# A second expert layer over pairs of batches: seven block products in place of eight

## The chip, the cores and the metric

The kernel runs on one core of one Trainium2 chip. The metric is the device time of one execution in microseconds (us), from the hardware profiler; lower is better. TensorE is called PE (its weight loads PEld), VectorE DVE, ScalarE ACT, GpSimd POOL; SP is the engine whose queue issues nearly all transfers (DMA).

## What is computed

```python
def _attn_ref(q, k, v, g_q, g_k):            # batch 4, heads 12, seq 448, head_dim 64
    q_n, k_n = (rmsnorm(q, g_q), rmsnorm(k, g_k))
    scores = scale * np.matmul(q_n, k_n.transpose(0, 1, 3, 2))
    scores = scores - np.max(scores, axis=-1, keepdims=True)
    attn = np.exp(scores)
    attn = attn / (np.sum(attn, axis=-1, keepdims=True) + 1e-09)
    return np.matmul(attn, v).astype(np.float32)

def _moe_ref(x, w_in, w_out):                # x 1792 x 768, w_in 768 x 2048, w_out 2048 x 768
    h = x @ w_in
    relu6 = np.clip(h + 3.0, 0.0, 6.0)
    g = h * relu6 / 6.0
    return (g @ w_out).astype(np.float32)

def _moe2_ref(x, w_in, w_out):               # the same sizes
    h = x @ w_in
    r = np.maximum(h, 0.0)
    g = r * r
    return (g @ w_out).astype(np.float32)

def reference(**kwargs):
    attn_out = _attn_ref(**attn_kwargs)
    x = np.ascontiguousarray(attn_out.transpose(0, 2, 1, 3)).reshape(B * S, H * D)
    x = _moe_ref(x=x, **moe_kwargs)
    return _moe2_ref(x=x, **moe2_kwargs)
```

The four weight matrices are float64; q, k, v and the result are float32.

## The kernel before, in words

**Numbers.** A product in the two layers is made to float32's precision by float16 matmuls. Both operands are multiplied by a power of two and split into a high and a low float16 part, and each product is three matmuls: high by high, high by low, low by high (L1017 to L1019). One such matmul takes a 128x128 block of weights and 448 columns, the tokens of one batch; the text calls it a *layer matmul*. There are 4608 of them.

**Weights.** `convert` (L867) takes a row of blocks of a weight matrix: it loads the float64 words (tile `wr`, L882), and makes float32 of them (tile `wf`) by five instructions: the sign (L902), the high word (L890 on ACT or L894 on DVE), the low word (L899), the join (L906) and the largest value (L913 on ACT or L909 on DVE). `scale_of` (L329) takes the largest over the partitions by a PE transpose (L341), eight small DVE instructions (L338 to L356) and a PE outer product (L350); the text calls this a *scale chain*. Then the row is split into high (L937, L940) and low (L944), tile `ws`. The first batch that needs a row uses it straight from `ws`; it is also stored to DRAM (`spill`, L947), and the other three batches load it from there (`again`, L960).

**Units.** `units()` (L38) lists the PE's work for the two layers: for each layer m and batch b, 16 units "in" (one 128-wide block row of h, 18 matmuls each) and 18 units "out" (three for each of the six block rows of the result, 18, 15 and 15 matmuls). The last six "out" units of a batch stand behind the "in" units of the next. A unit's position n in this list is the key of its tasks, and what it needs gets keys slightly below n.

**Around a unit.** `gate` (L1042) reads h from PSUM and makes g: for the first layer L1054 and L1060, for the second relu (L1056, ACT) and square (L1066 on ACT or L1063 on DVE). Once the 16 rows of a batch are there, `factors` (L1084) makes one scale for g and splits it (L1116 on ACT or L1119 on DVE, then L1122 on DVE). `result_y` (L1151) reads the first layer's result y, splits it to float16, puts it to DRAM (`kept`, L1191), and gets it back as `yk` (L1194) when the second layer starts. `result` (L1200) reads the second layer's result and stores it.

**Order.** `Plan` (L106) holds every task with its key, the engines that may do it with a cost for each, the tasks it waits for and the tiles it uses. `order` (L129) runs through time with these costs and writes one fixed program for each engine; `tc.manual_schedule()` (L1233) issues it in that order. Tiles live in classes of slots (`CLASSES`, L77; PSUM's eight banks are class `ps`). `STEPS`, `SCALE`, `VMAX`, `LOOK` and `LOOK0` shift the keys of the attention and of the preparation.

**Course.** Attention of batch 0 comes first; then the first layer of batch b, with the attention of batch b+1 beside it; then the second layer of batches 0 to 3. The second layer's weights are prepared while its batch 0 runs.

Of the kernel before, what the change touches and what calls it, by code (L numbers as in the profile page):

```python
# [9 lines left out]
F32 = mybir.dt.float32  # L10
# [39 lines left out]
UNITS = units()  # L50
# [26 lines left out]
CLASSES = {"A": 13, "H": 52, "B": 3, "wr": 3, "w": 8, "ps": 8}  # L77
# [197 lines left out]
def tile_kernel(ctx: ExitStack, tc: tile.TileContext, qk, v, vn, g, ident, w1i, w1o, w2i, w2o, out):  # L275
    nc = tc.nc

    def pool(name, bufs, **kw):
# [16 lines left out]
        "wf": ("w", 5, 5, [P, NW], F32), "ws": ("w", 6, 6, [P, 2, KC, P], F16),  # L295
        "ps_s": ("ps", 4, 5, [P, 512], F32), "ps_a": ("ps", 2, 3, [P, 512], F32), "ps_r": ("ps", 1, 1, [P, 512], F32), "ps_c": ("ps", 1, 2, [P, 512], F32), "ps_m": ("ps", 2, 3, [P, 512], F32),
# [22 lines left out]
    kept = dram.tile([B, KC, P, 2, S], F16, name="kept")  # L319
    spill = dram.tile([2 * (FC + KC * 3), P, 2, NW], F16, name="spill")  # L320
# [8 lines left out]
    def scale_of(key, name, vals, deps):  # L329
# [536 lines left out]

    def convert(m, i0, ns):  # L867
# [4 lines left out]
        vals, t_fs, t_ms = [], [], []  # L872
        for x, (i, n) in enumerate(zip(ids, ns)):
# [6 lines left out]
            def load(kind=kind, row=row, f0=f0, nf=nf, nw=nw, vwr=vwr):  # L880
                src = (w1i, w2i)[m][row] if kind == "in" else (w1o, w2o)[m][row][:, f0:f0 + nf]
                nc.sync.dma_start(tl(vwr)[:, 0:2 * nw], src.rearrange("p k c -> p (k c)").bitcast(I32))  # L882

            def words(vwr=vwr, nw=nw):
                x_ = tl(vwr).rearrange("p (c w) -> p c w", w=2)
                return x_[:, 0:nw, 0], x_[:, 0:nw, 1]

            def dx_a(words=words):
                x_ = words()[1].bitcast(F32)
                nc.scalar.activation(x_, x_, AF.Copy, scale=2.0 ** -112)  # L890

            def dx_v(words=words):
                x_ = words()[1].bitcast(F32)
                nc.vector.tensor_scalar(x_, x_, 2.0 ** -112, None, op0=ALU.mult)  # L894

            def d1(words=words, vwf=vwf, nw=nw):
                l_ = words()[0]
                low = tl(vwf).bitcast(U8).rearrange("p (c w) -> p c w", w=4)[:, 0:nw, 0]
                nc.scalar.activation(low, l_.bitcast(U32), AF.Copy, scale=2.0 ** -29 * (1 - 2.0 ** -9), bias=-0.49)  # L899

            def sign(words=words, vwf=vwf, nw=nw):
                nc.vector.tensor_scalar(tl(vwf)[:, 0:nw].bitcast(I32), words()[1], -(1 << 31), None, op0=ALU.bitwise_and)  # L902

            def join(words=words, vwf=vwf, nw=nw):
                w = tl(vwf)[:, 0:nw].bitcast(I32)
                nc.vector.scalar_tensor_tensor(w, words()[1], 3, w, op0=ALU.logical_shift_left, op1=ALU.bitwise_or)  # L906

            def most(vwf=vwf, nw=nw, x=x):
                nc.vector.tensor_reduce(mx[:, x:x + 1], tl(vwf)[:, 0:nw], axis=AX.X, op=ALU.max, apply_absolute_value=True)  # L909

            def sum_a(words=words, vwr=vwr, vwf=vwf, nw=nw, x=x):

                nc.scalar.activation(tl(vwr).bitcast(F32)[:, 0:nw], tl(vwf)[:, 0:nw], AF.Abs, accum_out=mx[:, x:x + 1])  # L913
# [3 lines left out]
            t_2 = task(kc, [("DVE", dve1(nw), sign)], [t_l], [vwr, vwf])  # L917
# [359 lines left out]
```

## Time and profile before

| | |
|---|---|
| three runs | 1176.98, 1178.19, 1178.38 us (median 1178.19) |
| span of the profiled execution | 1177.7 us; the page gives no other time for that execution |
| PE busy | 1108.0 us (94%), 6070 matmuls |
| DVE busy | 729.9 us (62%) |
| ACT busy | 690.8 us (59%) |
| POOL busy | 98.1 us (8%) |
| DMA | 231.18 MB, mean 196 GB/s |
| the chain that ended last | PE 72%, DVE 13%, ACT 8%, DMA 5%, issue 2% |

Busy shares are means over the whole span. Six stretches of it are told apart in the text, by the first layer matmul on new data: the first layer of batch 1 starts on PE at 287.70 us, of batch 2 at 432.70, of batch 3 at 581.90; at 656.90 PE takes the first gated values of batch 3; at 696.70 the first `yk` of the second layer (batch 0), at 818.00 that of batch 1, and the end is at 1177.70. The matmuls' own durations overlap, so the pace of PE is read from long runs of them in the chain, not from the mean of one.

### The profile page before, as it was taken

What the parts mean: (1) busy time and instruction counts of PE and PEld (TensorE: products, weight loads), DVE (VectorE), ACT (ScalarE), POOL (GpSimd) and SP (SyncE); (2) the same over time, 40 slices, a digit from 0 to 9 for tenths busy, and PEclk for the clock granted to TensorE, in tenths of its full rate; (3) what the DMA queues carried; (4) which work ended last, traced back from release to release, by engine and by line L of the source; (5) the groups of instructions that cost most, each with busy time, mean ns of one, the idle gap of its engine ahead of it and who ended that gap; (6) DMA issues with size and microseconds to landing.
All of it is one profiled execution on the core that took longest, in us unless ns stands there. A gap on an engine that the chain in (4) does not pass through costs nothing.

```text
span 1177.7 us, 17027 instructions
## 1 busy us (share of the span) xinstructions
PE 1108.0 (94%) x6070; PEld 573.7 (49%) x6070; DVE 729.9 (62%) x1676; ACT 690.8 (59%) x1353; POOL 98.1 (8%) x142
## 2 busy tenths in 40 slices
PE   0789999799999998999999998989999999999998
PEld 0455555355554444554555544544555555555554
DVE  7999899999899968899335657696144002100300
ACT  2799799996788846787223658784464034113400
POOL 3421211101111111210000000000000000000000
PEclk9999999899999999999999999999999999999999
DMA  9866567779989899998833767759636434454351
GB/s 239 216 185 196 151 190 235 242 158 310 305 199 231 212 251 244 224 210 207 206 107 117 261 219 281 276 180 319 226 128 201 161 113 135 132 157 121 90 164 54
DMA packets 214742, 231.18 MB, mean 196 GB/s; under 512 B 137872, under 2 KB 174864, under 8 KB 214656
## 3 DMA queue, kind: packets, MB, share of 16 engines
q1 hardware_dynamic: 214592, 229.95, 68.5%
q8 instruction: 48, 0.79, 0.3%
q14 instruction: 38, 0.31, 0.1%
q0 software_dynamic: 64, 0.13, 0.1%
HBM read 156.47 MB, written 36.18 MB: 164 GB/s over the span
## 4 chain that ended last, share of the span: by engine, by line
PE 72%; DVE 13%; ACT 8%; DMA 5%; issue 2%; POOL 0%; SPq 0%; DVEq 0%; ACTq 0%
PE m L1018 60%; PE ps_s L697 4%; DVE g L1122 2%; PE ps_a L793 2%; PE ps_a L774 2%; PE ps_s L667 2%; ACT wf L899 2%; DVE ws L944 2%; DVE nm L704 1%; PE ps_r L760 1%; ACT e L657 1%; DMA wr<-in_w2i_dram 1%; ACT wr L890 1%; ACT wr L913 1%; DMA qk<-in_qk_dram 1%
## 5 line engine op out<-in xcount | busy, mean ns | idle before, releaser
L1018 PEld LDWEIGHTS <-ws 128*128 128x128 f16 x4608 | 446.4, 98 | 430.3 <-issue 15.7
L1018 PE MATMUL m<-g,ws 128*128 128x448 f16 x2304 | 457.3, 354 | 7.6 <-DVE ws L944 3.8
L1018 PE MATMUL m<-x,ws 128*128 128x448 f16 x1152 | 232.7, 353 | 2.2 <-DVE ws L944 0.8
L1018 PE MATMUL m<-yk,ws 128*128 128x448 f16 x1152 | 224.4, 354 | 0.2 <-DVE ws L944 0.2
L657 ACT ACTIVATE e<-ps_s,nm,esc 128x448 f32<-128x448 f32 x168 | 122.1, 729 | 18.0 <-DVE nm L714 17.4
L704 DVE TENSOR_REDUCE nm<-ps_s 128x1 f32<-128x448 f32 x168 | 102.0, 612 | 3.4 <-PE ps_s L697 3.3
L1056 ACT ACTIVATE t<-m,inv 128x448 f32<-128x448 f32 x64 | 39.7, 624 | 98.5 <-PE m L1018 98.5
L1205 ACT ACTIVATE o<-m,ov 128x448 f32<-128x448 f32 x24 | 14.5, 631 | 137.4 <-PE m L1018 137.4
L1054 ACT ACTIVATE t<-m,half,six 128x448 f32<-128x448 f32 x64 | 46.0, 724 | 56.1 <-PE m L1018 56.1
L902 DVE TENSOR_SCALAR wf<-wr 128x768 int32<-128x768 int32 (+1 forms) x68 | 35.7, 529 | 60.2 <-PE m L1018 42.2
L906 DVE SCALAR_TENSOR_TENSOR wf<-wr,wf 128x768 int32<-128x768 int32 (+1 forms) x68 | 61.4, 906 | 12.6 <-ACT wf L899 11.9
L899 ACT ACTIVATE wf<-wr 128x768 uint8<-128x768 uint32 (+1 forms) x68 | 68.7, 1015 | 0.9 <-DVE wf L902 0.8
L697 PE MATMUL ps_s<-T,W 128*128 128x448 f16 (+1 forms) x192 | 61.9, 368 | 4.1 <-DMA W<-W_0r 3.8
L944 DVE SCALAR_TENSOR_TENSOR ws<-wf,w_s,ws 128x768 f16<-128x768 f32 (+1 forms) x68 | 64.7, 961 | 1.0 <-ACT ws L937 0.9
L1063 DVE SCALAR_TENSOR_TENSOR gr<-t 128x448 f32<-128x448 f32 x10 | 6.2, 622 | 95.3 <-ACT t L1056 95.2
L667 PE MATMUL ps_s<-eye,e 128*112 128x128 f32 x308 | 50.3, 297 | 15.7 <-ACT e L657 15.4
L890 ACT ACTIVATE wr<-wr 128x768 f32<-128x768 f32 (+1 forms) x52 | 45.1, 867 | 33.3 <-DVE wf L902 33.3
L697 PE MATMUL ps_s<-T 128*128 128x448 f16 (+1 forms) x192 | 62.5, 374 | 1.6 <-ACT e L657 0.9
L1060 DVE SCALAR_TENSOR_TENSOR gr<-t,m 128x448 f32<-128x448 f32 x64 | 39.1, 614 | 38.3 <-ACT t L1054 38.0
L338 DVE TENSOR_REDUCE g_s<-gm 128x1 f32<-128x16 f32 x4 | 0.7, 164 | 95.8 <-ACT gr L1066 95.6
L734 DVE SCALAR_TENSOR_TENSOR p<-e,su,p 128x448 f16<-128x448 f32 x91 | 59.1, 674 | 0.6 <-DMA ws<-spill 0.2
L913 ACT ACTIVATE wr<-wf 128x768 f32<-128x768 f32 (+1 forms) x62 | 50.3, 813 | 11.2 <-DVE wf L906 11.1
(199 smaller groups left out, 1268.9 us busy)
## 6 DMA issues: line engine op xcount, KB each, us to landing
ws<-spill SPq DMA_DIRECT2D x132, 384.0 KB, 3.7
ws<-spill SPq DMA_DIRECT2D x72, 320.0 KB, 3.7
spill<-ws SPq DMA_DIRECT2D x44, 384.0 KB, 4.2
wr<-in_w1i_dram SPq DMA_DIRECT2D x16, 768.0 KB, 5.2
wr<-in_w2i_dram SPq DMA_DIRECT2D x16, 768.0 KB, 6.0
qk<-in_qk_dram SPq DMA_DIRECT2D x23, 448.0 KB, 4.9
wr<-in_w1o_dram SPq DMA_DIRECT2D x12, 640.0 KB, 4.8
spill<-ws SPq DMA_DIRECT2D x24, 320.0 KB, 4.1
```

The lines of the kernel that those rows point to most:

```text
L657: nc.scalar.activation(tl(ve)[:, r % 2], tl(vps)[:, 0:S], AF.Exp, bias=sums["nm"][:, r:r + 1], scale=esc, accum_out=sums["su"][:, r:r + 1])
L667: nc.tensor.transpose(o[:, c], tl(ve)[:, r % 2, c * VR:(c + 1) * VR], eye)
L697: nc.tensor.matmul(ps[at:at + z - a, 0:S], q_[:, a:z], ks[:, h * S:(h + 1) * S], start=(i == 0), stop=(i == 1))
L704: nc.vector.tensor_reduce(sums["nm"][:, r:r + 1], tl(vps)[:, 0:S], axis=AX.X, op=ALU.max, negate=True)
L734: nc.vector.scalar_tensor_tensor(tl(vp)[:, r % 2, 1], tl(ve)[:, r % 2], sums["su"][:, r:r + 1], tl(vp)[:, r % 2, 0], op0=ALU.mult, op1=ALU ...
L890: nc.scalar.activation(x_, x_, AF.Copy, scale=2.0 ** -112)
L899: nc.scalar.activation(low, l_.bitcast(U32), AF.Copy, scale=2.0 ** -29 * (1 - 2.0 ** -9), bias=-0.49)
L906: nc.vector.scalar_tensor_tensor(w, words()[1], 3, w, op0=ALU.logical_shift_left, op1=ALU.bitwise_or)
L913: nc.scalar.activation(tl(vwr).bitcast(F32)[:, 0:nw], tl(vwf)[:, 0:nw], AF.Abs, accum_out=mx[:, x:x + 1])
L944: nc.vector.scalar_tensor_tensor(tl(vws)[:, 1, 0:nf].rearrange("p k c -> p (k c)"), tl(vwf)[:, 0:nw], up, hi, op0=ALU.mult, op1=ALU.subtract)
L1018: nc.tensor.matmul(tl(vph)[:, 0:S], w[:, wa, k], tl(rhs[k])[:, xa], start=(first_ and k == 0 and c == 0), stop=(last and k == nf - 1 and c ...
L1054: nc.scalar.activation(tl(vt), tl(vph)[:, 0:S], AF.Relu, bias=half, scale=six[:, row:row + 1])
```

## The change

The first layer stays as it was. The second layer works on two batches at once, (0, 1) and (2, 3). A weight matrix is cut into four blocks, A11, A12, A21, A22 (halves of its rows and of its columns), and the data into B11, B12, B21, B22 (halves of the inner dimension, and the two batches). Four blocks of the result need eight block products if each is made by itself. The change makes them from seven products of sums: S1 = A21+A22, S2 = S1-A11, S3 = A11-A21, S4 = A12-S2, and T1 = B12-B11, T3 = B22-B12, T2 = B22-T1, T4 = B21-T2. The products are 1: A11·B11, 2: A12·B21, 3: S4·B22, 4: A22·T4, 5: S1·T1, 6: S2·T2, 7: S3·T3.

- **Weights** (`sums`): two rows of blocks are loaded and made float32 as before (`words_of`, the same five instructions), one scale chain serves both, four additions (L1051) make the sums, and the seven pieces are split into high (L988, L992) and low (L996) and stored to DRAM (`spill_i`, `spill_o`). Every use loads them from there (L1107, L1117), the first one too. The keys run from 91.9 on, 3.27 apart for the first matrix and 2.43 for the second.
- **Data**: y is put to DRAM as float32, `combine` gets it back (L1346), makes the four differences (L1378) and splits the seven operands (L1360, L1366). `split_g` does the same for g (L1518, then L1502 or L1505, and L1508).
- **Products**: `pair_in` (L1465) takes 9 matmuls for a product of one row pair, `pair_out` (L1555) 24, in three rows. `accumulate` leaves sums of products in PSUM: bank A takes products 1, 6, 7, 4 one behind the other, B takes 2, C takes 5 and 3. After each product the bank is read (L1404 on ACT, L1407 on DVE, L1410 with an addition on DVE) before the next goes into it. The rows of `pair_in` are interleaved: 1, 2 and 5 of row 0, 1 and 2 of row 1, 6 of row 0, 5 of row 1, 7 of row 0, 1 and 2 of row 2, 6 of row 1, 4 of row 0, and so on.
- **Gates**: L1478 on DVE, or L1481 and L1482 on ACT, in place.
- **Order**: the in-products of pair 0, the last six "out" units of the first layer (`LEFT`), the out-products of pair 0 (all but product 2), the in-products of pair 1, product 2 of pair 0, the out-products of pair 1. `STEPS`, `SCALE`, `VMAX`, `LOOK`, `LOOK0` and two slot counts have new values.

```diff
@@ units() @@
-    for m in range(2):
-        for b in range(B):
-            seq += [(b, m, i) for i in INS]
...
+    for b in range(B):
+        seq += [(b, 0, i) for i in INS]
...
+    return seq, [(left, 0, i) for i in OUTS[-TAIL:]]
+UNITS, LEFT = units()
+PAIRS = ((0, 1), (2, 3))
+IN_ORDER = (1, 2, 6, 5, 7, 4, 3)
+OUT_ORDER = ((1, 5, 6, 7, 4, 3, 2), (1, 5, 6, 2, 7, 4, 3))
+PARTS = ((0, 3), (3, 3), (6, 2))
+FROM, EVERY, SOON = 91.90176350071762, (3.2666303583830514, 2.425499875163164), 3.9296033978343754
@@ sums(kind, r, keys) @@
+        up, down, t_u, t_d = scale_of(key, f"w2_{name}", lambda: mx, t_ms, SHIFT)
...
+            t_12 = split(.0, a11, 1, [t_f[0]], nw=2 * nq)
+            t_22 = split(.15, a22, 4, [t_f[1]])
+            t_s1 = add(.2, [t_22], a22, ALU.add, a21, a22)
+            t_5 = split(.25, a22, 5, [t_s1])
+            t_s3 = add(.3, [t_s1, t_f[0]], a21, ALU.subtract, a11, a21)
+            t_s2 = add(.35, [t_5, t_f[0]], a22, ALU.subtract, a22, a11)
+            t_6 = split(.4, a22, 6, [t_s2])
+            split(.45, a21, 7, [t_s3])
+            t_s4 = add(.5, [t_6, t_12], a22, ALU.subtract, a12, a22)
+            split(.55, a22, 3, [t_s4])
@@ accumulate @@
+        m1 = cells(1, va, True, [])
+        s1 = read(1, va, None, x11, [v11], [m1], False)
+        m2 = cells(2, vb, True, [])
+        e11 = read(2, vb, x11, x11, [v11], [m2, s1], True)
+        m6 = cells(6, va, False, [s1])
+        s2 = read(6, va, None, x12, [v12], [m6], False)
+        m7 = cells(7, va, False, [s2])
+        s3 = read(7, va, None, x22, [v22], [m7], False)
+        m4 = cells(4, va, False, [s3])
+        e21 = read(4, va, None, x21, [v21], [m4], False)
+        m5 = cells(5, vc, True, [])
+        e22 = read(5, vc, x22, x22, [v22], [m5, s3], True)
+        m3 = cells(3, vc, False, [e22])
+        e12 = read(3, vc, x12, x12, [v12], [m3, s2], True)
@@ the order of the calls @@
+    combine(0, N_IN)
+    pair_in(0, N_IN)
+    split_g(0, n_out)
+    combine(1, n_in)
+    pair_in(1, n_in)
+    pair_out(0, n_out, n_in + 31)
+    split_g(1, n_in + 35)
+    pair_out(1, n_in + 35, None)
```

Two places of the programs show what this moves. The first is ACT where the second layer's first in-units run. Before (`t` and `gr` are the gate's tiles, `wr`, `wf`, `ws` those of the weights):

```order
L1056 ACTIVATE t_7609<-m_7543,inv_1_182 128x448
L1066 ACTIVATE gr_7617,gm_1_183<-t_7609 128x448
L913 ACTIVATE wr_7519,wm_6_125<-wf_7562 128x768
L1056 ACTIVATE t_7634<-m_7571,inv_1_182 128x448
L937 ACTIVATE ws_7639<-wf_7541,w_4_s 128x768
L1066 ACTIVATE gr_7652,gm_1_183<-t_7634 128x448
```

Now (`mi_0A` is bank A of row 0, `gq` the results, `wq` and `wc` the float32 rows and the float16 pieces of the weights; row 803 of the program first):

```order
L1404 ACTIVATE gq_0_1_7953<-mi_0A,inv_0_176 128x448
L917 ACTIVATE wr_out_1_0_7713,w2m_out_111<-wq_out_1_7899 128x768
L988 ACTIVATE wc_in_0_2_7969<-wq_in_0_7557,w_in_s 128x384
L890 ACTIVATE wr_out_1_1_7823<-wr_out_1_1_7823 128x768
L988 ACTIVATE wc_in_0_1_7950<-wq_in_0_7557,w_in_s 128x384
L900 ACTIVATE wq_out_1_7899<-wr_out_1_1_7823 128x768
L1481 ACTIVATE gq_0_0_7882<-gq_0_0_7882 128x448
L1482 ACTIVATE gq_0_0_7882,gm_0_177<-gq_0_0_7882 128x448
L1404 ACTIVATE gq_1_0_8006<-mi_1A,inv_0_176 128x448
L917 ACTIVATE wr_out_1_1_7823,w2m_out_111<-wq_out_1_7899 128x768
L1404 ACTIVATE gq_0_3_8023<-mi_0A,inv_0_176 128x448
```

Between the reads of the same bank after product 6 and after product 7 now stand nine other instructions, six of them of the weights' preparation.

The second place is DVE where the splits of g start for the first out-products. Before (batch 1 of the second layer; the scale chain, then the splits):

```order
L346 TENSOR_SCALAR g_1_s<-g_1_s 1x1
L347 TENSOR_SCALAR g_1_s<-g_1_s 1x1
L356 COPY g_1_s<-g_1_p 128x2
L1137 TENSOR_SCALAR ov_1_198<-iwo_86,g_1_s 128x6
L1119 TENSOR_SCALAR g_1_1_10919<-gr_10535,g_1_s 128x448
L1122 SCALAR_TENSOR_TENSOR g_1_1_10919<-gr_10535,g_1_s,g_1_1_10919 128x448
```

Now (pair 0; `go_1_0` is g's operand for product 1, block 0):

```order
L361 TENSOR_SCALAR g_0_s<-g_0_s 1x1
L1051 TENSOR_TENSOR wq_out_0_8705<-wq_out_0_8705 128x384
L996 SCALAR_TENSOR_TENSOR wc_out_1_0_9040<-wq_out_1_8836,w_out_s,wc_out_1_0_9040 128x768
L996 SCALAR_TENSOR_TENSOR wc_out_0_1_9026<-wq_out_0_8705,w_out_s,wc_out_0_1_9026 128x384
L1532 TENSOR_SCALAR ov_0_182<-iw2o,g_0_s 128x3
L1051 TENSOR_TENSOR wq_out_0_8705<-wq_out_0_8705 128x384
L996 SCALAR_TENSOR_TENSOR wc_out_0_2_9066<-wq_out_0_8705,w_out_s,wc_out_0_2_9066 128x384
L1508 SCALAR_TENSOR_TENSOR go_1_0_9076<-gq_0_0_7882,g_0_s,go_1_0_9076 128x448
```

The last of the weights' sums and splits now stand among the first splits of g.

## Rows read from the trace of the kernel before

**Rows 1.** The page's busy time of each engine over the whole span.

```profile
PE 1108.0 (94%) x6070; PEld 573.7 (49%) x6070; DVE 729.9 (62%) x1676; ACT 690.8 (59%) x1353; POOL 98.1 (8%) x142
```

**Rows 2.** End of the chain that ended last: start, length, engine, tile, line, instructions.

```profile
886.72 106.80 PE m L1018 x564
995.07 107.93 PE m L1018 x570
1104.56 69.36 PE m L1018 x366
```

**Rows 3.** Six stretches: length, busy time of engines, PE's granted clock, DMA share, GB/s.

```profile
287.70:432.70 145.00, 143.06 (x809) 71.91 (x808) 133.14 (x312) 113.22 (x228) 21.14 (x30) 1.00 0.96 243
432.70:581.90 149.20, 145.38 (x820) 72.32 (x819) 120.26 (x273) 94.02 (x198) 19.19 (x30) 0.99 0.97 216
581.90:656.90 75.00, 74.69 (x406) 38.37 (x404) 32.54 (x62) 23.02 (x38) 0.00 (x0) 1.00 0.47 155
656.90:696.70 39.80, 38.54 (x205) 19.78 (x203) 21.62 (x51) 19.41 (x30) 0.00 (x0) 1.00 0.67 227
696.70:818.00 121.30, 112.78 (x575) 56.27 (x574) 97.99 (x235) 92.89 (x162) 0.00 (x0) 0.97 0.73 256
818.00:1177.70 359.70, 355.78 (x1882) 183.84 (x1880) 55.62 (x127) 110.28 (x224) 0.00 (x0) 1.00 0.45 144
```

**Rows 4.** What PE waited for, 656 to 820 us: total, times, longest wait.

```profile
PE w_p L350 <- DVE w_s L347: 2.5, 3, 1.9
PE w_p L341 <- DVE w_s L338: 2.3, 3, 1.1
PE m L1018 <- ACT ws L937: 2.3, 1, 2.3
PE m L1018 <- DVE ws L944: 1.7, 3, 0.8
```

**Rows 5.** Groups of instructions by shape: busy time, mean ns of one; idle before.

```profile
L902 DVE TENSOR_SCALAR wf<-wr 128x768 int32<-128x768 int32 x44 | 24.2, 553 | 23.3 <-PE m L1018 10.9 <-DMA wr<-in_w2o_dram 6.9 <-DMA wr<-in_w2i_dram 3.6
L906 DVE SCALAR_TENSOR_TENSOR wf<-wr,wf 128x768 int32<-128x768 int32 x44 | 41.8, 954 | 8.9 <-ACT wf L899 8.3
L944 DVE SCALAR_TENSOR_TENSOR ws<-wf,w_s,ws 128x768 f16<-128x768 f32 x44 | 44.2, 1008 | 0.0
L488 DVE TENSOR_TENSOR qk<-qk,gg 128x448 f32<-128x448 f32 x24 | 14.7, 614 | 0.1
L1122 DVE SCALAR_TENSOR_TENSOR g<-gr,d,g 128x448 f16<-128x448 f32 x64 | 38.8, 671 | 0.0
L1056 ACT ACTIVATE t<-m,inv 128x448 f32<-128x448 f32 x64 | 39.7, 624 | 98.5 <-PE m L1018 98.5
```

**Rows 6.** DVE's timeline at 641 us: start, length, engine, line, operation.

```profile
641.25 0.17 DVE L338 TENSOR_REDUCE g_s<-gt 128x1 f32<-128x16 f32 x1
641.78 0.28 DVE L344 TENSOR_REDUCE g_s<-g_p 1x1 f32<-1x128 f32 x1 [0.36 <-PE g_p L341]
642.10 0.14 DVE L323 TENSOR_SCALAR g_s<-g_s 1x1 int32<-1x1 int32 x1
...
643.23 0.16 DVE L356 COPY g_s<-g_p 128x2 f32<-128x2 f32 x1 [0.58 <-PE g_p L350]
...
644.18 9.62 DVE L1122 SCALAR_TENSOR_TENSOR g<-gr,d,g 128x448 f16<-128x448 f32 x16
```

**Rows 7.** Four short stretches, columns as in rows 3.

```profile
218.00:222.00 4.00, 0.65 (x4) 0.40 (x4) 4.00 (x8) 4.00 (x9) 2.14 (x5) 0.98 0.78 234
222.00:226.00 4.00, 2.47 (x9) 1.09 (x9) 3.52 (x13) 4.00 (x10) 0.00 (x0) 0.50 0.50 172
230.00:234.00 4.00, 3.32 (x16) 1.49 (x14) 4.00 (x8) 4.00 (x9) 0.00 (x0) 0.74 0.99 349
804.00:808.00 4.00, 4.00 (x23) 2.08 (x22) 3.40 (x5) 2.71 (x5) 0.00 (x0) 1.00 1.05 412
```

**Rows 8.** Transfers by the page: queue, count, KB each, us from issue to landing.

```profile
ws<-spill SPq DMA_DIRECT2D x132, 384.0 KB, 3.7
spill<-ws SPq DMA_DIRECT2D x44, 384.0 KB, 4.2
```

More of the change, by code (lines that the diff above doesn't have):

```diff
@@ L888, in dx_a @@
[L888 to L899, printed above, removed]
@@ L952, in convert, with halve, ends, hi_a @@
             stored[m, i] = task(n - LOOK0[2] + .2, [("SP", 600, store)], [t_l], [vws], xfer=nf * 182)
+    iw2i, iw2o = lasting(QI, "iw2i"), lasting(QO, "iw2o")
+    cells_at, gated = [], []
+    stored_i, stored_o, wscale_i, wscale_o = {}, {}, {}, {}
+    def halve(key, part, at, nw, vws, to, up, deps, uses):
+        def ends():
+            t, w = part()[0][:, at:at + nw], tl(vws).rearrange("p a k c -> p a (k c)")
+            return t, w[:, 0, to:to + nw], w[:, 1, to:to + nw]
+        def hi_a():
+            x, hi, _ = ends()
+            nc.scalar.activation(hi, x, AF.Copy, scale=up)
+        def hi_v():
+            x, hi, _ = ends()
+            nc.vector.tensor_scalar(hi, x, up, None, op0=ALU.mult)
+        def lo():
+            x, hi, l = ends()
+            nc.vector.scalar_tensor_tensor(l, x, up, hi, op0=ALU.mult, op1=ALU.subtract)
+        t_h = plan.task(key, [("ACT", act(nw, 90), hi_a), ("DVE", dve1(nw) + 60, hi_v)], deps, [vws, *uses])
+        return plan.task(key + .1, [("DVE", dve2(nw) + 60, lo)], [t_h], [vws, *uses])
@@ L970, in tile_kernel @@
     last_mm = [None]
-    pos = {u: n for n, u in enumerate(UNITS)}
+    N_IN = len(UNITS)
+    N_LEFT = N_IN + 4 * 7 * QI // 8 + 3
+    pos = {u: n for n, u in enumerate(UNITS)} | {u: n + N_LEFT for n, u in enumerate(LEFT)}
     def in_table(b, m, n):
@@ new lines, in chain @@
+    def chain(split, minus, b11, b12, b21, b22, d11, d12, d21, d22):
+        t_1 = split(.5, b11, 1, [d11])
+        t_t1 = minus(.6, b11, b12, b11, [t_1, d12])
+        t_2 = split(.65, b21, 2, [d21])
+        t_t3 = minus(.7, b12, b22, b12, [t_t1, d22])
+        t_5 = split(.75, b11, 5, [t_t1])
+        t_t2 = minus(.8, b11, b22, b11, [t_5, d22])
+        t_6 = split(.85, b11, 6, [t_t2])
+        split(.9, b12, 7, [t_t3])
+        t_t4 = minus(.95, b21, b21, b11, [t_2, t_6])
+        split(1.0, b21, 4, [t_t4])
+        split(1.05, b22, 3, [t_t2, t_t3])
@@ new lines, in tile_kernel, with taken, a_, v_ @@
+    put_y, y_op, y_done = {}, {}, {}
+    graw, gsum, g_op, g_done = {}, {}, {}, {}
+    scale2, tab2 = {}, {}
+    def taken(key, vph, src, dst, c, t, add):
+        def a_():
+            nc.scalar.activation(dst(), tl(vph)[:, 0:S], AF.Copy, scale=c)
+        def v_():
+            nc.vector.tensor_scalar(dst(), tl(vph)[:, 0:S], c, None, op0=ALU.mult)
+        def plus():
+            nc.vector.scalar_tensor_tensor(dst(), tl(vph)[:, 0:S], c, src(), op0=ALU.mult, op1=ALU.add)
+        if add:
+            return [("DVE", dve2(S) + 60, plus)]
+        return [("ACT", act(S, 50), a_), ("DVE", dve2(S) + 60, v_)]
@@ L1220, in tile_kernel @@
             attention(b, p, STEPS[b][p], SCALE[b])
+    at = FROM
+    for q in range(QI):
+        sums("in", q, [at])
+        at += EVERY[0]
+    for r in range(QO):
+        sums("out", r, [at + EVERY[1] * x for x in range(len(PARTS))])
+        at += EVERY[1] * len(PARTS)
     own = {b: set() for b in range(B)}
     seen = set()
-    for n, (b, m, i) in enumerate(UNITS):
+    for n, (b, m, i) in enumerate(UNITS + LEFT):
         if (m, i) not in seen:
@@ L1231, in tile_kernel @@
         unit(b, m, i, n)
+    for n, u in enumerate(LEFT):
+        unit(*u, N_LEFT + n)
+    n_out = N_LEFT + len(LEFT)
+    n_in = n_out + 24
+    combine(0, N_IN)
[6 more added lines that the diff above has]
+    pair_out(1, n_in + 35, None)
+    cells_at.sort(key=lambda x: x[0])
+    for n, late in gated:
+        t = next(t for k, t in cells_at if k >= n)
+        t.after.append(late)
+        late.left += 1
     emit = plan.order()
```

374 lines of the change are left out of this document (296 added, 78 removed).

## The prediction

> **What bounds the kernel now.** I read the busy shares first, then the chain that ended last, then the stretches, then PE's waits. PE is busy 1108.0 us of 1177.7; DVE and ACT stand at 62% and 59% [rows 1]. The chain ends in three long runs of layer matmuls: 106.80 us for 564, 107.93 for 570, 69.36 for 366 [rows 2], so PE's pace is .1894 us a matmul. The stretches [rows 3] show three regimes. Beside attention (287.70 to 581.90) PE is busy 143.06 of 145.00 and 145.38 of 149.20 us, with DVE at 133.14 and 120.26: PE and DVE are both nearly full. From 581.90 to 696.70 and from 818.00 on PE is full and DVE has room: 55.62 busy in the last 359.70. Between lies the one leaky stretch, 696.70 to 818.00, where the second layer's weights are prepared: 537 layer matmuls and 24 short ones need 537 x .1894 + 4.9 = 106.6 us (a short one some .2), and it lasted 121.3, so 14.7 are lost with DVE busy only .81 of the time (97.99 of 121.30). The named waits there [rows 4] go to the scale chain (2.5 and 2.3) and to weight pieces not ready (2.3 and 1.7): a late preparation, not a late transfer.
>
> So from 581.90 on the end is set by PE's count of matmuls, and by how well DVE's preparation hides beside them.
>
> **Before 581.90: 0.** The change takes the same layer matmuls through the first layer. Summed by row durations, DVE's instructions up to the 1632nd layer matmul need 510.9 us after and 510.3 before, PE's 476.8 and 475.3. The new keys move attention and weights among themselves; I bound this by 5 us either way, about the 3.8 us (149.20 - 145.38) that PE was not busy in the second attention stretch [rows 3].
>
> **Matmuls removed.** By the two programs, layer matmuls fall from 4608 to 4320 (2304 in layer 1, 1008 in, 1008 out): -288 x .1894 = -54.5 us, all from the part where PE is the bound. From 581.90 on 2697 are left of 2976: 9 of the 288 are a shift of the anchor, since after it more first-layer matmuls stand behind the third batch's first one. They take 510.8 us; 32 scale-chain matmuls take 6.6 and the tail behind the last matmul 3.8 as before (1177.7 - 1173.9, [rows 2]). **Floor: 581.9 + 510.8 + 6.6 + 3.8 = 1103.1 us**, if PE never waits.
>
> **DVE's work, moved forward and grown.** Until the second pair's first in-product, PE has 1599 layer matmuls and 30 short ones, 309 us. Beside these DVE now has, from its program (means of [rows 5], less .07 for instructions back to back, since 16 splits of mean .671 took 9.62 us, .60 each [rows 6]; .00105 us a column by the widths 448 and 768):
>
> - the second layer's weights: 34 rows, as many columns as 32 of 768. Signs 32 x .48 = 16, joins 32 x .88 = 28; 102 lows, 14 groups of one 768 wide (.94) and five 384 wide (.53) and 3 of 512 and 256, 58; 68 sums at the rate of the 448-wide tensor-tensor row (.614), 31; high parts that fall to DVE 11. Sum 144.
> - 15 scale chains: .17 + .28 + 4 x .14 + .16 = 1.2 by their own times, about 1.0 overlapped [rows 6]: 15.
> - the first layer's last batch: 16 gates and 22 maxima at .55, 16 lows at .60, small ones: 33.
> - y's operands: 35 lows at .60 and 20 differences at .55: 32.
> - reads of PSUM with addition (27), plain (5), gates (9): 26.
> - g's operands: 56 lows, 32 differences, 3 highs: 52.
>
> Together 302 us of DVE beside 309 of PE. ACT has 260 by the same kind of sum. Before, the work on the same stretch was loose, but for 696.70 to 818.00. How densely can DVE be filled? The nearest row is the first attention stretch, .92 busy (133.14 of 145.00) while PE went on at 143.06 [rows 3]; there too the planner mixed chains of DVE, ACT and PE. At .92 the 302 need 328 us: **+19**. At the .81 of the leaky stretch they need 373: +64. Below, nothing: 0. I take .92 because the preparation now starts some 45 units earlier and is spread over three stretches; at .81 each weight was made just before its use.
>
> **Weights through DRAM.** The first use now loads too. From the third batch's start to `LEFT` the program issues 67.2 MB over some 208 us, 323 GB/s. The chip moved 412 in 804 to 808 [rows 7], and 256 at share .73 [rows 3], which at full share would be 351: the queue carries it, closely. 0, with a few us above. The last weight row is the exception: its sums and splits stand among the first splits of g, and its piece has to be stored (4.2 us) and loaded (3.7) [rows 8], 7.9 us where the two rows of matmuls ahead give 48 x .1894 = 9.1 less the splits still missing: **+3**, from 0 to 8.
>
> **Reads between products.** A product goes into a bank after the bank has been read: 88 such handovers, with at least 9 matmuls (1.70 us) of another bank between. A read takes .624 [rows 5]. ACT's queue is tight in the first in-products: from the end of row 0's product 6 until product 4 starts PE has 45 matmuls, 8.5 us, and ACT between its reads about 7 us of other work, with two reads 8.3. Covered, if DVE and ACT run on time. In the second half (g's second split with 6 matmuls as cover for the first operands, DVE and ACT otherwise loose) I take **+4**, from 0 to 8.
>
> Sum: 1103.1 + 19 + 3 + 4 = **1129 us**. The profiled span, 1177.7, is .5 below the median of the runs and inside their 1.4, so it stands for them.
>
> **Rivals.**
>
> *Hardly any loss, 1104 to 1112, at 1107.* For: DVE and ACT were under 33 us in the 75.00 from 581.90 and under 22 in the 39.80 after [rows 3], so the new work fills holes. Against: 302 of 309 leaves no slack, and .92 is the densest that a long stretch showed. Chance .20.
>
> *Weights late as before, 1145 to 1175.* The same chains that cost 14.7 us in 121.3 [rows 4] now last over 309: at .81 it is 1103.1 + 64 + 4 = 1171. Against: what PE waits for is no longer made just before its use. Chance .15.
>
> *Slower by the handovers, 1180 and more.* The products of one bank wait on a read by ACT or DVE, and these have weights in their queues. PE would stop briefly at each, and its clock could fall: after the pause at 218 to 222 (PE busy .65 of 4.00) the granted clock was .50, which is 1.2 GHz, then .74 at 230 to 234 before it was full again; at 222 to 226 PE's busy 2.47 us held 9 matmuls, where a full stretch holds 23 in 4.00 [rows 7]. To end above the time before, the loss over the floor must be 75 us: .85 at each of 88 handovers, so a read done 1.70 + .85 = 2.55 us behind the product's end, four times the read's .624. Against: a read stands ahead of later preparation by its key, and the leaky stretch, with its waits, still had .97 [rows 3]. The Trainium skill speaks for this rival (TensorE: Matmul & The Clock Gate, "A second HAM failure mode: psum-queue depth-cycling"): a kernel that cycles through PSUM banks lets PE idle briefly between groups, so that its clock goes up and down and the throughput falls although single matmuls look fast. The trace agrees that the clock falls behind a pause; that banks alone do it no row here shows. Chance .08.
>
> *The change doesn't do what it says:* the programs count 4320 layer matmuls, so this has no chance; that losses eat all the gain to within .2% of the time before (2.4 us, what a measurement can tell here) gets .02.
>
> **Chances and range.** Forecast, 1115 to 1145: .55. With the rivals .20, .15, .08 and .02. Faster is .55 + .20 + .15 = .90. The range leaves out some of the lowest tenth and most of the late case: from 1106 (the floor and a few us) to 1162 (about half of the loss at .81), which holds 8 in 10.
>
> **What would show it.** Right: layer matmuls 288 fewer, still .1894 apart in long runs; DVE over .85 busy between the third batch's first matmul and the last out-unit of layer 1, with PE's lost time there, some 15 to 25 us, behind DVE's weights, gates and splits; PE at 97% or more in the last 190 us; a clock of .95 or more in each stretch. Wrong: PE's largest waits on the reads L1404, L1407, L1410 in the second half, where DVE is loose, or a clock under .9 there (handovers); waits on transfers of pieces (the DRAM detour); the first 580 us changed by more than 5 us (the new keys); or hardly any wait at all (the planner filled DVE better than .92).

## The result and the profile after

The changed kernel takes **1141.91 us** (median of 4 runs, 1140.2 to 1143.22) where the kernel before took 1177.86 on the same chip: ratio .9699, 95% interval .9681 to .9717. The forecast was 1129, the range 1106 to 1162. It is faster, and 12.9 us slower than forecast.

The changed kernel's span and busy time of each engine, from its page:

```profile
span 1140.9 us, 17129 instructions
...
PE 1053.7 (92%) x5761; PEld 544.9 (48%) x5761; DVE 905.0 (79%) x1977; ACT 793.7 (70%) x1544; POOL 95.9 (8%) x142
```

PE's busy time fell by 54.3 us [rows 1], as 288 matmuls at .1894 should. The shares of the chain that ended last, from the same page:

```profile
PE 50%; DVE 21%; ACT 15%; DMA 10%; issue 3%; SPq 0%; POOL 0%; ACTq 0%; DVEq 0%
```

It runs through PE for 50% where it was 72%: PE waits more often than before.

The stretches of the changed kernel, with the columns of [rows 3]. The borders are the same events: first layer matmul of batch 1, 2 and 3 (batches counted from 0; "the third batch" of the prediction and of the first expectations, "the fourth" in later ones, is batch 3), then the first in-product of pair 1 (927.77) and the first matmul of product 2 of pair 0's out-products (1023.12). The last two rows begin at the same border. The stretch from batch 3's start to the first in-product of pair 1 is called the *long stretch* below.

```profile
0.00:286.85 286.85, 234.66 (x1344) 130.62 (x1345) 260.37 (x604) 236.65 (x467) 56.74 (x82) 0.96 0.73 206
286.85:438.88 152.03, 147.69 (x823) 73.34 (x822) 137.51 (x316) 112.24 (x224) 22.91 (x36) 1.00 0.99 239
438.88:595.91 157.03, 148.15 (x851) 73.64 (x850) 121.27 (x273) 91.43 (x191) 16.24 (x24) 0.98 0.97 225
595.91:927.77 331.86, 314.62 (x1645) 159.63 (x1644) 304.39 (x646) 256.93 (x472) 0.00 (x0) 1.00 0.80 270
927.77:1023.12 95.35, 95.35 (x504) 49.33 (x505) 18.45 (x28) 53.75 (x119) 0.00 (x0) 1.00 0.40 126
927.77:1140.90 213.13, 208.56 (x1101) 107.64 (x1101) 81.43 (x142) 96.44 (x194) 0.00 (x0) 1.00 0.38 125
```

The kernel before, up to batch 1:

```profile
0.00:287.70 287.70, 237.74 (x1382) 131.24 (x1383) 268.74 (x620) 237.95 (x478) 57.77 (x82) 0.98 0.74 209
```

Read against [rows 3], this says where the forecast missed. Batch 3 starts at 595.91 and not at 581.90: **14.0 us are lost in the first layer's part, which I had taken as unchanged.** Added up over the three stretches ahead of batch 3, PE is idle for 65.4 us where it was idle for 55.7, which is 9.7 of the 14.0, and busy for 530.5 where it was busy for 526.2, with a granted clock of .96 for .98 ahead of batch 1. (22 matmuls of attention more and 9 layer matmuls fewer stand ahead of the border.) From there to the end it takes 545.0 us where the forecast had 1129 - 581.9 = 547.1. The long stretch was to take 309 + 19 + 3 = 331 and took 331.86; the rest was to take 216 and took 213.13. Even DVE's 304.39 us are the 302 of the sum, at a share of .917. Whether this is for the reasons given, the experiments have to say.

The six longest of the waits that the profile names for PE from 595 to 928 us (columns as in [rows 4]):

```profile
PE m L1177 <- DMA ws<-spill: 2.7, 3, 1.6
PE w_in_p L364 <- DVE w_in_s L361: 2.5, 2, 1.5
PE mi_4A L1465 <- DMA spill_o<-wc_out: 2.2, 1, 2.2
PE w_in_p L355 <- DVE w_in_s L352: 1.4, 1, 1.4
PE mi_1C L1465 <- DMA wi<-spill_i: 1.1, 1, 1.1
PE mo_0C L1555 <- DMA wo<-spill_o: 1.1, 1, 1.1
```

Over all sixteen named waits, transfers end 9.4 us and DVE's scale chains 5.8; splits and reads come to 1.9. (The 2.2 us are put down to a store, which an in-product does not read, so that line is not to be trusted in detail.) That is not what the forecast's DVE term would show. The transfers of that stretch (issue lines: queue, count, KB each, median us to landing) point to a reason:

```profile
wr_in<-in_w2i_dram SPq DMA_DIRECT2D x14, 768.0 KB, 6.7
wi<-spill_i SPq DMA_DIRECT2D x28, 384.0 KB, 5.0
ws<-spill SPq DMA_DIRECT2D x19, 384.0 KB, 4.3
```

A 384 KB piece needs 5.0 us here; the reloads before, over their whole program, needed 3.7 [rows 8].

### The profile page after: what moved, and what is told of

Read it like the earlier page. It is cut to its first block, busy times and chain, and to the rows that moved or that the text cites. A ratio compares the mean times of both kernels' runs of the same rounds, so it can differ in the third digit from the quotient of the medians.

```text
span 1140.9 us, 17129 instructions
## 1 busy us (share of the span) xinstructions
PE 1053.7 (92%) x5761; PEld 544.9 (48%) x5761; DVE 905.0 (79%) x1977; ACT 793.7 (70%) x1544; POOL 95.9 (8%) x142
## 4 chain that ended last, share of the span: by engine, by line
PE 50%; DVE 21%; ACT 15%; DMA 10%; issue 3%; SPq 0%; POOL 0%; ACTq 0%; DVEq 0%
PE m L1177 17%; PE ps_s L711 3%; PE ps_s L681 2%; PE ps_a L788 2%; PE mo_1A L1555 2%; PE mo_0A L1555 2%; PE ps_a L807 2%; PE mo_2A L1555 2%; DMA spill_i<-wc_in 2%; DVE nm L718 2%; ACT e L671 2%; PE mo_2C L1555 1%; PE ps_r L774 1%; DVE wc_out L996 1%; DMA spill_o<-wc_out 1%
## 5 line engine op out<-in xcount | busy, mean ns | idle before, releaser
L1177 PEld LDWEIGHTS <-ws 128*128 128x128 f16 x2304 | 221.4, 98 | 219.2 <-issue 13.1
L1177 PE MATMUL m<-g,ws 128*128 128x448 f16 x1152 | 235.6, 355 | 6.5 <-DVE ws L966 3.5
L1465 PEld LDWEIGHTS <-wi 128*128 128x128 f16 x1008 | 98.2, 98 | 99.9 <-issue 6.1
L1555 PEld LDWEIGHTS <-wo 128*128 128x128 f16 x1008 | 98.2, 98 | 96.3 <-DMA wo<-spill_o 2.9
L1502 ACT ACTIVATE go<-gq,g_s 128x448 f16<-128x448 f32 x105 | 63.3, 659 | 39.5 <-DVE gq L1518 28.2
L1508 DVE SCALAR_TENSOR_TENSOR go<-gq,g_s,go 128x448 f16<-128x448 f32 x112 | 70.8, 674 | 0.2
L681 PE MATMUL ps_s<-eye,e 128*112 128x128 f32 x308 | 51.6, 304 | 16.7 <-ACT e L671 16.7
L742 ACT ACTIVATE p<-e,su 128x448 f16<-128x448 f32 x70 | 44.5, 663 | 17.7 <-DVE su L657 9.5
L464 POOL TENSOR_TENSOR rs<-ss,mhalf 128x14 f32<-128x14 f32 x21 | 54.8, 2611 | 1.8
L1219 DVE SCALAR_TENSOR_TENSOR gr<-t,m 128x448 f32<-128x448 f32 x64 | 39.0, 612 | 10.9 <-ACT t L1213 10.8
L1481 ACT ACTIVATE gq<-gq 128x448 f32<-128x448 f32 x55 | 31.4, 571 | 21.2 <-DVE gq L1410 20.7
L1555 PE MATMUL mo_0A<-go,wo 128*128 128x448 f16 x192 | 42.1, 352 | 1.6 <-DVE go L1508 1.6
L1555 PE MATMUL mo_1A<-go,wo 128*128 128x448 f16 x192 | 41.5, 352 | 0.0
L1555 PE MATMUL mo_2A<-go,wo 128*128 128x448 f16 x192 | 40.9, 353 | 0.1
```

Source lines behind the costliest of these rows:

```text
L464: nc.gpsimd.tensor_tensor(r, ss, mhalf, op=ALU.pow)
L681: nc.tensor.transpose(o[:, c], tl(ve)[:, r % 2, c * VR:(c + 1) * VR], eye)
L1177: nc.tensor.matmul(tl(vph)[:, 0:S], w[:, wa, k], tl(rhs[k])[:, xa], start=(first_ and k == 0 and c == 0), stop=(last and k == nf - 1 and c ...
L1465: nc.tensor.matmul(tl(vph)[:, 0:S], w[:, wa, k0 + k], tl(vo)[:, to, xa], start=(starts and k == 0 and x == 0), stop=(k == KH - 1 and x == ...
L1502: nc.scalar.activation(tl(vo)[:, 0], tl(v_), AF.Copy, scale=up)
L1508: nc.vector.scalar_tensor_tensor(tl(vo)[:, 1], tl(v_), up, tl(vo)[:, 0], op0=ALU.mult, op1=ALU.subtract)
```

## The experiments

Three questions were open: what made the first part late, what holds PE in the long stretch, and whether handovers between banks cost anything. In all but three runs (the new keys in the kernel before, and the two new orders) the order of the changed kernel is kept, and single instructions in it are cut, repeated or moved to another engine. Times are single runs but for the change's, the median of four, and those with an interval; "before" is the kernel before on the same chip.

| run | us | before | batch 3 starts | from there to pair 1 |
|---|---|---|---|---|
| the change | 1141.9 | 1177.9 | 595.9 | 331.9 |
| x1_no_sums | 1134.3 | 1179.1 | 593.3 | 326.0 |
| x2_pieces_half | 1128.5 | 1179.1 | 592.5 | 321.1 |
| x6_both | 1121.2 | 1177.2 | 591.0 | 315.3 |
| x7_no_pe_chain | 1141.1 | 1177.2 | 593.9 | 332.4 |
| x8_all_three | 1118.2 | 1177.2 | 593.2 | 310.1 |
| x9_sums_on_pool | 1148.1 | 1182.2 | 591.6 | 341.7 |
| x3_reloads_half | 1136.0 | 1179.1 | 592.6 | 328.4 |
| x5_reads_thrice | 1146.4 | 1177.2 | 588.2 | 333.2 |

All nine rows have one order in the first part, and batch 3 starts between 588.2 and 595.9: that is how far one execution differs from another there. The profile shown of the change is the latest of them, so its lateness against the one profile of the kernel before is 14.0 us, and 6 to 14 over these runs. How far the start of the kernel before varies was not measured. The long stretch varies less: 331.9 and 333.2 in the two runs that leave it alone (the change, x5).

### Was it DVE, or the transfers? x1 and x2

x1, every sum on one column (the same for y's and g's differences):

```diff
-                    nc.vector.tensor_tensor(d, x_, y_, op=op)
+                    nc.vector.tensor_tensor(d[:, 0:1], x_[:, 0:1], y_[:, 0:1], op=op)
```

> The changed kernel with its order kept, and every sum of operands (68 of the second layer's weights, 24 of y, 64 of g) made on one column where it was 256 to 448: the sums themselves are left out of the computation. Theory DVE: the 24 us that PE loses after the third batch's first matmul come from filling DVE densely. DVE falls by about 59 us, 302 to some 250 beside PE's 309, so the stretch from the third batch's first matmul to the second pair's first in-product (331.9 us, 595.9 to 927.8) shrinks to 309 to 316, and the time by 16 to 22, to 1119 to 1126. Rival transfers: the loss comes from the DMA share of .88 to .89 in 596 to 830; then the stretch stays above 328 and the time above 1137. Neither moves the first 596 us by more than 2.

x2, high halves only (the same at `spill_o`):

```diff
-            nc.sync.dma_start(tl(vws).rearrange("p a k c -> p a (k c)")[:, :, 0:size], spill_i[q, t][:, :, 0:size])
+            nc.sync.dma_start(tl(vws).rearrange("p a k c -> p a (k c)")[:, 0, 0:size], spill_i[q, t][:, 0, 0:size])
...
-                            nc.tensor.matmul(tl(vph)[:, 0:S], w[:, wa, k0 + k], tl(vo)[:, to, xa], start=(starts and k == 0 and x == 0), stop=(k == KH - 1 and x == 2), skip_group_check=True)
+                            nc.tensor.matmul(tl(vph)[:, 0:S], w[:, 0, k0 + k], tl(vo)[:, to, xa], start=(starts and k == 0 and x == 0), stop=(k == KH - 1 and x == 2), skip_group_check=True)
```

> The changed kernel with its order kept; of the second layer's weight pieces only the high halves are stored to and loaded from DRAM, and the matmuls with a low weight take the high one instead (the low halves are left out of the products). Same matmuls, same DVE and ACT work, about half the bytes of the pieces (some 24 MB less until the second pair's first in-product). Theory DVE: that stretch (331.9 us) shrinks by 0 to 4. Rival transfers: it shrinks by 12 or more, to under 320.

The long stretch without the sums:

```profile
593.32:919.35 326.03, 314.04 (x1646) 159.53 (x1644) 259.20 (x647) 257.40 (x472) 0.00 (x0) 1.00 0.82 275
```

and with half of the pieces' bytes:

```profile
592.53:913.62 321.09, 313.41 (x1645) 160.03 (x1644) 303.19 (x646) 255.71 (x472) 0.00 (x0) 1.00 0.64 211
```

Taking 45 us off DVE (304.39 to 259.20) brought 5.9 of the 16 or more that the DVE theory wanted. Halving the bytes brought 10.8 with DVE as loaded as ever (303.19 of 321.09, a share of .944). The waits that name transfers fell from 9.4 us to .5. So **.92 was no limit of DVE**, and the larger part of the loss hung on transfers, which the forecast had put at nothing. Both theories are half wrong: x2's 10.8 also stays under the 12 that its own theory wanted.

### Do the losses add? x6, x7, x8

x6 is x1 and x2 together. x7 keeps PE out of the weights' scale chains (`own` is set for the second layer's weights):

```diff
-            nc.tensor.transpose(tl(vps)[0:1, 0:P], m, eye)
+            if not own:
+                nc.tensor.transpose(tl(vps)[0:1, 0:P], m, eye)
```

> No sums and half of the pieces' bytes at once, order kept (both left out of the computation as in the two runs alone). The stretch from the fourth batch's first matmul to the second pair's first in-product was 331.9 us, 326.0 without the sums, 321.1 with half the bytes; PE needs 309. If the two are separate losses, they add: 313 to 317. If they are the same loss (late weights by either road), it stays at 319 to 322.

> The changed kernel with its order kept; the eleven scale chains of the second layer's weights make their scale from each partition's own largest value and take nothing from PE (the largest over the partitions is left out), so PE never stands at their two short matmuls with layer matmuls behind. The waits named there are 4.8 us in all. Theory blocked PE: the same stretch shrinks by 4 to 7, to 325 to 328. Rival: PE then waits as long at the next late piece, and the stretch shrinks by under 2.

> No sums, half of the pieces' bytes and no PE in the weights' scale chains, order kept. If these three are the whole loss, the stretch comes to PE's own need, 307 to 311 us. If over 314 remains, something else holds PE there, such as the first layer's own reloads.

Measured: 315.3 for both, which is the sum of the two gains (5.9 + 10.8 = 16.7 off 331.9 gives 315.2). The scale chains alone gave nothing (332.4), though the profile names 4.8 us of waits there. In x7 PE came earlier to the next place that waits for DVE, the scale chain of the last g of the first layer, and stood there for 5.6 us where the changed kernel stands 1.0:

```profile
PE g_p L357 <- DVE g_s L353: 5.6, 1, 5.6
```

Behind this pause, between 652 and 664 us, the granted clock was .78, and reads of products held PE for 6.1 us in the long stretch of x7 where they hold it for 1.1 in the changed kernel. So the waits moved to DVE's chain and to reads, and not to a late piece, as the expectation's rival had it. The long stretch in x6 and in x8:

```profile
591.03:906.32 315.29, 311.42 (x1646) 160.51 (x1644) 259.18 (x647) 255.83 (x472) 0.00 (x0) 1.00 0.65 215
```

```profile
593.15:903.22 310.07, 305.50 (x1613) 157.45 (x1612) 257.92 (x647) 255.17 (x472) 0.00 (x0) 1.00 0.67 219
```

In x6 PE idles 3.9 us where it idled 17.2 in the changed kernel (331.86 - 314.62): sums and bytes are nearly the whole loss. x8's 310.1 lies in the expected range, but the short matmuls it leaves out are PE's own work (busy 305.50 for 311.42), so that PE's own need is 305 there and its idle time, 4.6, is no less than in x6. The 5.2 us that x8 gained over x6 are this work, which counts where PE is the bound; in x7 the same cut was worth nothing.

### Can GpSimd take the sums? x9

```diff
-                    nc.vector.tensor_tensor(d, x_, y_, op=op)
+                    nc.gpsimd.tensor_tensor(d, x_, y_, op=op)
```

> The changed kernel, whole and with its order kept on every other engine: the 68 sums of the second layer's weights and the 24 differences of y are made on GpSimd, which stands idle from 596 us on, where DVE made them. DVE falls by 40 us or so in the stretch from the fourth batch's first matmul to the second pair's first in-product (331.9 us). Leaving these and g's differences out altogether took 7.6 us off the time. Theory DVE: 3 to 7 us come off, 1135 to 1139. Rival: GpSimd's sums are slow and lie on the chain of a weight row, sum after sum, so the pieces come later than before and the time grows, to 1144 or more.

1148.1 us on a chip where the kernel before took 1182.2, a ratio of .971 against the change's .970: no gain, and the stretch grew to 341.7. The groups by shape, first GpSimd's sums and two of DVE's groups from 594 to 926 us in this run:

```profile
L1051 POOL TENSOR_TENSOR wq_in<-wq_in 128x384 f32<-128x384 f32 x32 | 39.6, 1236 | 139.0 <-DMA ws<-spill 80.1 <-DVE wc_in L996 54.9 <-DVE w_in_s L352 2.0
L911 DVE SCALAR_TENSOR_TENSOR wq_out<-wr_out,wq_out 128x768 int32<-128x768 int32 x12 | 13.8, 1155 | 1.7 <-ACT wq_out L900 1.5
L1508 DVE SCALAR_TENSOR_TENSOR go<-gq,g_s,go 128x448 f16<-128x448 f32 x53 | 42.5, 841 | 0.6
```

and the same three in the changed kernel:

```profile
L1051 DVE TENSOR_TENSOR wq_in<-wq_in 128x384 f32<-128x384 f32 x32 | 17.5, 548 | 0.0
L911 DVE SCALAR_TENSOR_TENSOR wq_out<-wr_out,wq_out 128x768 int32<-128x768 int32 x12 | 11.4, 951 | 0.5 <-ACT wq_out L900 0.3
L1508 DVE SCALAR_TENSOR_TENSOR go<-gq,g_s,go 128x448 f16<-128x448 f32 x56 | 35.7, 674 | 0.0
```

A sum takes 1236 ns on GpSimd and 548 on DVE, and DVE's own instructions with two tensor operands take longer in this run, 1155 ns for 951 and 841 for 674. DVE gave away 49 us of sums in the long stretch, and its busy time there fell by 7 (304.4 to 297.4, in a stretch that was 9.8 longer). PE's named waits on scale chains, which DVE makes, grew from 5.8 us to 9.7, those on transfers fell from 9.4 to 7.1. So the gain failed at least in part because DVE slowed down; that the pieces came later, as the expectation's rival says, is not shown.

### Do handovers between banks cost? x5

```diff
+            for _ in range(times):
-            nc.scalar.activation(dst(), tl(vph)[:, 0:S], AF.Copy, scale=c)
+                nc.scalar.activation(dst(), tl(vph)[:, 0:S], AF.Copy, scale=c)
```

with `times` 3 in pair 1, and the same on DVE.

> The changed kernel with its order kept; each plain read of a product of the second pair (44 of them, L1404 on ACT or L1407 on DVE) is made three times, 1.25 us more on the way from a product's end to the next product of its bank. Theory covered: the 1.70 us of another bank's matmuls between hide a read of .62 and nearly hide three (1.9): the time grows by 0 to 12. Rival handovers: if reads were already on PE's path, the 33 reads with a product behind them would cost 1.25 each, over 35 in all, and the clock in the last 213 us would fall under .95.

Pair 1's part in this run:

```profile
921.32:1144.60 223.28, 210.00 (x1101) 107.57 (x1101) 80.92 (x142) 149.03 (x282) 0.00 (x0) 1.00 0.36 119
```

Pair 1 took 223.28 us where it had taken 213.13 (the whole grew by 4.5, since in this execution batch 3 started 7.7 earlier): 10.2 for reads that would have cost 33 x 1.25 = 41 on PE's path, and the clock stayed at 1.00. Of the 10.2, 8.7 are named as waits on reads, 1.0 or so each. Single reads are covered: in 927.77 to 1023.12 above, PE is busy all of the 95.35 us, through 56 products in three banks a row. The Trainium skill's rule on this (TensorE: Matmul & The Clock Gate, "A second HAM failure mode: psum-queue depth-cycling") does not show here: PE went from bank to bank all the time without an idle moment, at a clock of 1.00, and even the idle 13.3 us of x5's last part left the clock there.

### What made the first part late? x3 and x4

x3 halves the bytes of the first layer's reloads in the way of x2; x4 puts the change's STEPS, SCALE, VMAX and LOOK0 into the kernel before and changes nothing else.

> The changed kernel with its order kept; the first layer's weights are reloaded without their low halves, and a reloaded unit's matmuls with a low weight take the high one instead (left out of the product). This takes some 16 MB from the transfers before the third batch's first matmul, which lies 14 us later than in the kernel before. Theory transfers in the first part: with a DMA share of .97 to .99 from 287 to 596 us that stretch is bound by transfers, and 3 MB more moved before the third batch made it late; then its first matmul comes at 586 or earlier. Rival order: the new keys put attention's DVE, ACT and PE work in a worse order, transfers or not; then it stays at 592 to 598.

> The kernel before with the change's values of STEPS, SCALE, VMAX and LOOK0 and nothing else. Theory keys: the new keys alone make the first part late, so the third batch's first matmul comes at 592 to 600 (581.9 before), with the second layer as it was, and the whole takes 1185 to 1210. Rival new work: the keys cost nothing, and the second layer's early weight loads and its tiles made the first part late; then the third batch starts at 578 to 586.

The two stretches of batches 1 and 2 in x3:

```profile
286.15:439.30 153.15, 149.30 (x823) 73.68 (x822) 137.99 (x317) 112.85 (x224) 23.09 (x36) 0.99 0.88 205
439.30:592.60 153.30, 147.33 (x851) 74.40 (x850) 120.81 (x272) 90.68 (x190) 16.22 (x24) 0.98 0.78 179
```

and in x4:

```profile
287.11:440.76 153.65, 149.19 (x816) 73.98 (x815) 133.33 (x309) 106.86 (x211) 19.67 (x30) 0.98 0.90 231
440.76:604.76 164.00, 153.57 (x871) 77.31 (x869) 132.75 (x304) 99.73 (x212) 20.36 (x30) 0.98 0.94 212
```

In x3 the share of the transfers fell from .97 to .78 in the third stretch and batch 3 started at 592.6, inside the spread of the runs that keep all bytes. So a DMA share of .97 to .99 did not make that part late, as far as this spread lets one see. In the long stretch, which holds reloads of the first layer too, x3 gained 3.5 us (328.4). In x4 the old second layer follows, and yet batch 3 starts at 604.8 and the whole takes 1199.8 us (before: 1179.1). So **the new keys alone make the first part late**, by more than they do in the changed kernel. Which of the keys does it was not tried, nor were the changed `LOOK` and the two slot counts.

### How much is order worth? x10 and x11

Both kernels issue their tasks from a list in place of the planner's result; tasks, tiles and slots stay, and a task that may run on ACT or DVE may change sides.

```diff
+ORDER = (
...
+)
...
-        return out
+        return [self.tasks[int(x[:-1])].ways['abc'.index(x[-1])][2] for x in ORDER.split()]
```

> The changed kernel with the same tasks and tiles in another order, on each engine, and some of the tasks that may run on ACT or DVE on the other of the two; the order was made with the durations of the traces and with 3.1 us for a transfer from the end of its bytes to its use, where the planner has 1.5. Theory order: what PE waits for is work that was ready to be done elsewhere but stood in a wrong place; the time falls by 40 us or more, to 1065 to 1100, with the fourth batch's first matmul at 570 or earlier. Rival: DVE, ACT and the transfers are full as they are, and no order helps; then it stays above 1130.

> The kernel before, its order made anew in the same way. Theory count: seven products instead of eight are worth their 288 matmuls, 54.5 us, where both orders are equally good; then this one lies 45 to 60 above the changed kernel with its new order. Rival: the seven products bring so much work to DVE, ACT and the transfers that an equally good order leaves less than 40 of it.

The changed kernel in its new order takes **1095.53 us** (4 runs, 1095.16 to 1096.62; ratio to before .9319, interval .9303 to .9334). The kernel before in its new order takes 1149.38 (1148.88 to 1152.62; ratio .9781, interval .9766 to .9797). The difference is **53.9 us**, and 288 matmuls at .1894 are 54.5. The two orders are about equally good: in their profiles PE is idle for 54.3 us in the changed kernel (1094.0 - 1039.75) and for 49.8 in the kernel before (1147.3 - 1097.54), and busy for 57.8 less. An agreement to within 1 us is partly luck; one to within some 5 is shown. Batches 1, 2, then batch 3 to pair 1, then the rest, in the changed kernel's new order:

```profile
269.67:422.08 152.41, 152.41 (x881) 76.96 (x879) 141.21 (x327) 123.21 (x255) 30.02 (x38) 1.00 1.04 254
422.08:568.39 146.31, 146.31 (x848) 73.69 (x847) 122.20 (x292) 89.39 (x193) 14.51 (x23) 1.00 0.98 231
568.39:880.67 312.28, 309.49 (x1635) 159.57 (x1634) 294.86 (x621) 246.27 (x466) 0.00 (x0) 1.00 0.85 285
880.67:1094.00 213.33, 209.53 (x1108) 108.22 (x1106) 122.68 (x244) 47.31 (x93) 0.00 (x0) 1.00 0.40 131
```

Of the 46.4 us, 27.5 lie ahead of batch 3's start (568.4 for 595.9) and 19.6 in the long stretch (312.3 for 331.9). All sums, bytes and scale chains are still there, DVE busy .944 of the stretch and the transfers at .85, and PE is busy 309.49 of 312.28. A 384 KB piece still needs 4.9 us to land there. Neither DVE nor the transfers had been full; their work had stood in places from which it came late.

## Why the prediction was right, and where it was not

**Matmuls removed, -54.5: right.** PE's busy time fell by 54.3, and with equally good orders the two kernels differ by 53.9.

**Before 581.90, "0 ... by 5 us either way": wrong, and by the profile this is the whole miss.** Equal sums of durations on both sides were taken for equal time. Batch 3 started 14.0 us later in the profile (6 to 14 over the runs), which with 2.1 gained later and 1.0 between profile and median makes the 12.9. The prediction had named a change of more than 5 us here as a sign of being wrong. The new keys do it by themselves (x4), by order, and not by the bytes of the reloads (x3). I had summed PE's and DVE's work up to the 1632nd layer matmul, but PE's idle time, 9.7 us more of it, is set by the order, and no such sum holds it.

**DVE's work, 302 us: right. "+19" at .92: the number came out by luck, the reason did not.** The long stretch took 331.86 for 331. But DVE can be at .944 there with PE busy for 309.49 of 312.28 us (x10), and taking 45 us of DVE away returned 5.9. What DVE's term had too much, the transfers' term had too little: the sums (x1) are worth 5.9 us and half of the bytes (x2) 10.8, together 16.7 of the 19. A share taken from another stretch is a description of that stretch's order, not a limit.

**Weights through DRAM, "0, with a few us above": mis-sized.** In this order half of the pieces' bytes are worth 10.8 us of the long stretch. Waits on transfers of pieces were the second sign of being wrong that the prediction had named, and they were seen. I compared means (323 GB/s wanted, 351 there) and took a queue that is nearly full for one that doesn't delay; pieces landed after 5.0 us in place of 3.7. It is a loss of this order all the same, since x10 moves every byte, its pieces land after 4.9, and it loses 2.8 us in all. That the last row of pieces costs 3 was not tried alone; near the first out-product PE's named waits are .8 on g's split and 1.1 on a piece.

**Reads between products, covered: right.** In the long stretch two waits on a read are named, .7 and .4 us, and in pair 1 none. Even the tight place held. ACT's timeline there, with start and length:

```profile
730.87 0.61 ACT L1404 ACTIVATE gq<-mi_0A,inv 128x448 f32<-128x448 f32 x1
...
739.63 0.62 ACT L1404 ACTIVATE gq<-mi_0A,inv 128x448 f32<-128x448 f32 x1
```

These are the reads after row 0's products 6 and 7, 8.8 us apart. And PE's:

```profile
738.95 1.86 PE L1465 MATMUL mi_1A<-yo,wi 128*128 128x448 f16 x9
740.65 1.87 PE L1465 MATMUL mi_0A<-yo,wi 128*128 128x448 f16 x9
```

Product 4 starts at 740.65 without a wait, .4 us behind the second read's end. The +4 for the second half was .9: 213.13 where matmuls, short ones and tail need 212.2.

**The rivals.** "Weights late as before" was nearer than its chance of .15 said, but at a third of its price (23 of 64 lost). "Slower by the handovers" is refuted by the full 95.35 us and by x5. "Hardly any loss" is what the change could have been in another order: x10 lies 12 under the middle of that case, since its first part gains too.

## What to carry to other kernels

Where one list scheduler orders everything, a change of its keys is a change of the whole program, and a part whose instructions are the same need not take the same time: read the new order where PE meets the other engines, or give that part tens of microseconds of range (new keys alone moved batch 3's start by 22.9 here). To learn which resource binds, keep the order and cut one thing at a time, then two together; a share of .92 or .97 alone did not show a limit here. To learn what an algorithm is worth, compare both versions with orders of the same quality: here 53.9 us for 54.5 counted, where the first comparison showed 36.

## What the hardware showed that was not expected

GpSimd's sums slowed DVE. In x9, from 594 to 926 us, each DVE instruction can be sorted by whether a GpSimd instruction ran at the same time. Low halves of g (L1508) took 677 ns in the 38 cases without one and 1254 in the 15 with one; joins (L911, 768 wide) 954 and 1238. Reads of a product with an addition (L1410), which take one operand from PSUM, took 676 in both cases. Two low halves beside two of GpSimd's differences, with a low half of y just before them:

```profile
898.16 1.13 POOL L1378 TENSOR_TENSOR yu<-yu 128x448 f32<-128x448 f32 x1 [32.48 <-DVE yo L1366]
899.38 1.39 POOL L1378 TENSOR_TENSOR yu<-yu,yu 128x448 f32<-128x448 f32 x1
897.41 0.68 DVE L1366 SCALAR_TENSOR_TENSOR yo<-yu,y_s,yo 128x448 f16<-128x448 f32 x1
898.23 3.03 DVE L1508 SCALAR_TENSOR_TENSOR go<-gq,g_s,go 128x448 f16<-128x448 f32 x2
```

The Trainium skill has a rule for it (SBUF — State Buffer, "SBUF: two separate sides"): DVE and GpSimd share a pair of SBUF ports, and a DVE instruction with two SBUF inputs and a GpSimd instruction that reads SBUF exclude each other. The rows agree: only instructions that met one of GpSimd's grew, and those with an operand in PSUM did not. In one place they go beyond the rule as it is given here: signs (L907, 768 wide), which read a single tensor, took 555 ns without and 730 with a GpSimd instruction beside them (6 cases); no run here shows why.

The start of batch 3 also varies more than expected with the order unchanged: on one chip it came between 588.2 and 593.9 us in four runs (x5 to x8), while the whole time of the change lies within 3.0 us over four runs.
